# Batch 0's values loaded two rows to a partition and put in order by TensorE, in a fused sliding-window attention and feed-forward kernel

## The chip, the cores and the metric

The kernel runs on one core of a Trainium2 chip. The metric is the device time of one execution in microseconds (us). The engines are TensorE (PE in the profile; its weight loads are PEld), VectorE (DVE), ScalarE (ACT), GpSimd (POOL) and SyncE (SP), which here only issues DMAs. "SPq" is time that SP spends issuing a DMA.

## The reference

Eight batches of attention with eight heads, 576 positions and 64 values a head. A query sees keys at most 32 positions away. The result, with the heads side by side, is the input of a feed-forward block with a tanh-GELU.

```python
scores = (1/sqrt(64)) * q @ k.T                     # q, k, v: (8, 8, 576, 64) float32
scores = where(abs(pos_q - pos_k) <= 32, scores, -1e9)
attn = softmax(scores)                              # per batch and head
x = (attn @ v).transpose(0, 2, 1, 3).reshape(4608, 512)
h = x @ w_in                                        # w_in: (512, 2048)
out = gelu_tanh(h) @ w_out                          # w_out: (2048, 512)
```

## The kernel before

Heads are taken in pairs ("pair" below: heads 2g and 2g+1, g from 0 to 3), because two heads of 64 fill 128 partitions. The attention of a batch has four groups, one for each pair, and a fifth for the last positions. Everything is computed in float16 with float32 sums.

The feed-forward block works on 512 tokens at a time (stage t). Its input `xT` holds the attention's result transposed: 128 rows for each pair, so pair g of the attention is reduction block `dc = g` of the first product. `ffn_in(t, n, d0, d1)` multiplies column block n of w_in (16 blocks of 128) with reduction blocks d0 to d1; `gelu` follows; `ffn_out_0` does the second product of stage 0, in the order `ORDER_0`, 64 slots of one matmul each. While stage t runs its second product, the attention of batch t+1 is interleaved into it by slot number; for stage 0 the table is `PLAN_0`: "s" is a score, "r" a transposition of a pair, "n" sums and their inverse, "p" the product with the values, "x" the spread into xT, "w" and "u" casts of w_out's blocks, "d" shifted copies of V, "c" differences of w_out's blocks.

Queues are in order: each engine runs its instructions in the order in which the code emits them. The beginning, up to stage 0's second product, is written out by hand. SP issues nearly all loads in this order: q and k of batch 0 by pair, the tails of v (positions 512 to 575), v by head, and the eight blocks of w_in (`load_w_in(x, dc)`: half x of the columns, reduction block dc), with v's last two heads between the first blocks. Behind them come q and k of batch 1 and w_out. The loads of w_in and w_out go to five staging buffers of which batch 0's v takes one.

For batch 0 a pair goes through these steps:

- `cast_early` casts q and k, `turn` transposes both on TensorE, and `trans_out` copies them from PSUM to `QTs` and `KTs`. q and k are loaded four rows to a partition, so the keys are written with a step of four.
- `score` adds a bias of -30000 outside the window (`bias`, through matmuls with the identity `idn`), adds the scores, and takes the exponent on ACT.
- `sums_of` sums the exponents with a matmul, and ACT turns the sum into its inverse by a logarithm and an exponent (`invert`).
- `values` casts v of the pair from the load's buffer to `Vs` and `pair_v` makes two copies shifted by 64 positions, on DVE, since windows overlap two tiles of 128.
- `finish` multiplies with the values (`times`) and writes the product with the inverse to xT (`spread`).

`V` has position p of tile c at partition p, slot c, so v is loaded with one row of 64 float32 (256 bytes) for each descriptor. Between `finish(1)` and `finish(2)`, `spin` issues matmuls on a zeroed tile whose results are not used. Then `block_in` runs the first product of column blocks 0 to 5, one reduction block at a time, each after its cast (`cast_w_in`: half on POOL, half on ACT or DVE). `finish(3)` stands behind reduction block 1, and the ACT table for GELU is loaded after it.

w_out's blocks 12 to 15 are staged in two loads of two blocks. The action "w3" casts blocks 12 (DVE) and 13 (POOL) at slot 47, the action "u3" casts blocks 14 (POOL) and 15 (ACT) at slot 55. The second product reads blocks 12 and 13 from slot 48 and blocks 14 and 15 from slot 56.

## Time and profile before

| | us |
|---|---|
| median of 3 runs (lowest to highest) | 297.86 (296.98 to 298.21) |
| the profiled execution | 299.54 |
| its span, first to last instruction | 297.8 |
| TensorE busy in the span | 285.9 (96%) |
| VectorE, ScalarE, GpSimd busy | 212.8 (71%), 196.4 (66%), 89.3 (30%) |

The mean granted TensorE clock is 1.000. The chain of work that ended last is 85% TensorE, 6% DMA, 3% issues by SP and 2% VectorE. The kernel moves 51 MB; 98,471 of its 114,392 DMA packets are under 512 bytes. Times in the text are microseconds from the start of the span. A bracket behind an instruction in a listing gives the time that its engine stood idle before it, and what ended that.

### The profile page before, as it was taken

What the parts mean: (1) busy time and instruction counts of PE and PEld (TensorE: products, weight loads), DVE (VectorE), ACT (ScalarE), POOL (GpSimd) and SP (SyncE); (2) the same over time, 40 slices, a digit from 0 to 9 for tenths busy, and PEclk for the clock granted to TensorE, in tenths of its full rate; (3) what the DMA queues carried; (4) which work ended last, traced back from release to release, by engine and by line L of the source; (5) the groups of instructions that cost most, each with busy time, mean ns of one, the idle gap of its engine ahead of it and who ended that gap; (6) DMA issues with size and microseconds to landing.
All of it is one profiled execution on the core that took longest, in us unless ns stands there. A gap on an engine that the chain in (4) does not pass through costs nothing.

```text
span 297.8 us, 7286 instructions
## 1 busy us (share of the span) xinstructions
PE 285.9 (96%) x2945; PEld 192.6 (65%) x2945; DVE 212.8 (71%) x467; ACT 196.4 (66%) x315; POOL 89.3 (30%) x143
## 2 busy tenths in 40 slices
PE   7879999999999999999999999999999999999992
PEld 3434544557875687568855885588557867877781
DVE  4655378897897667868786878686857867865852
ACT  5965766778577875777667765786578558707700
POOL 3426315102347622305260615060800050024000
PEclk9999999999999999999999999999999999999999
DMA  7999999999999996999988999999693040013013
GB/s 231 235 327 412 353 310 221 257 183 193 268 240 195 262 219 130 146 130 242 163 191 132 251 117 191 111 244 155 118 147 42 2 130 12 2 36 109 0 55 89
DMA packets 114392, 51.02 MB, mean 171 GB/s; under 512 B 98471, under 2 KB 110247, under 8 KB 114102
## 3 DMA queue, kind: packets, MB, share of 16 engines
q1 hardware_dynamic: 89460, 38.67, 61.4%
q0 software_dynamic: 23776, 10.83, 23.3%
q10 hardware_dynamic: 1122, 1.06, 1.1%
q8 instruction: 23, 0.38, 0.6%
q14 instruction: 11, 0.09, 0.1%
HBM read 36.70 MB, written 9.44 MB: 155 GB/s over the span
## 4 chain that ended last, share of the span: by engine, by line
PE 85%; DMA 6%; SPq 3%; DVE 2%; ACT 1%; issue 0%; POOL 0%; ACTq 0%
PE mm L751 33%; PE ph L577 17%; PE mm L577 17%; PE ps_s L468 3%; PE pu L629 3%; DMA wst<-in_moe_w_in_dram 2%; PE ps_d L495 2%; DMA KT<-k 2%; PE mm L723 2%; PE py L723 2%; PE ps_o L505 2%; SPq L271 2%; DMA qr<-in_q_dram 1%; PE mm L629 1%; PE ps_od L495 1%; SPq L246 1%
## 5 line engine op out<-in xcount | busy, mean ns | idle before, releaser
L577 PEld LDWEIGHTS <-w_in 128*128 128x128 f16 x512 | 57.4, 113 | 50.4 <-POOL w_in L250 2.1
L577 PE MATMUL ph<-xT,w_in 128*128 128x512 f16 x256 | 64.6, 379 | 1.1 <-POOL w_in L250 1.1
L577 PE MATMUL mm<-xT,w_in 128*128 128x512 f16 x256 | 64.1, 379 | 0.0
L713 POOL DMA_DIRECT2D out_dram<-y x55 | 32.3, 597 | 84.9 <-DVE y L780 76.2
L585 ACT ACTIVATE gT<-mm 128x512 f16<-128x512 f32 x60 | 35.6, 598 | 33.1 <-PE mm L577 32.5
L751 PEld LDWEIGHTS <-s 128*128 128x128 f16 x512 | 49.3, 98 | 7.1 <-DVE s L694 0.6
L751 PE MATMUL mm<-t,s 128*128 128x256 f16 x376 | 45.2, 273 | 0.2 <-DVE y L764 0.2
L694 DVE TENSOR_TENSOR s<-gT 128x512 f16<-128x512 f16 x64 | 27.8, 435 | 19.4 <-ACT gT L585 19.3
L751 PEld LDWEIGHTS <-gT 128*128 128x128 f16 x384 | 36.2, 98 | 6.4
L585 ACT ACTIVATE gT<-ph 128x512 f16<-128x512 f32 x58 | 32.4, 604 | 11.2 <-PE ph L577 11.2
L481 ACT ACTIVATE pe<-ps_s 128x960 f16<-128x960 f32 (+1 forms) x31 | 29.6, 976 | 13.4 <-PE ps_s L468 13.3
L751 PE MATMUL mm<-w_out,gT 128*128 128x256 f16 x256 | 32.6, 273 | 0.0
L104 ACT ACT_TABLE_LOAD x18 | 23.1, 1283 | 2.2 <-issue 1.9
L530 ACT ACTIVATE lt<-ps_d 128x480 f32<-128x480 f32 (+2 forms) x28 | 15.5, 555 | 11.4 <-PE ps_d L495 7.9
L531 ACT ACTIVATE lt<-lt 128x480 f32<-128x480 f32 (+3 forms) x36 | 21.1, 586 | 1.1
L490 DVE TENSOR_TENSOR pe<-pe,band 128x960 f16<-128x960 f16 x28 | 18.1, 664 | 2.1 <-ACT pe L481 2.0
L505 PEld LDWEIGHTS <-V 128*64 128x64 f16 x520 | 13.8, 111 | 6.4 <-DVE V L226 1.6
L751 PE MATMUL mm<-t,gT 128*128 128x256 f16 x128 | 16.2, 273 | 0.0
L216 POOL DMA_DIRECT2D V<-in_v_dram x16 | 14.4, 910 | 1.3 <-POOL after L989 0.4
L694 DVE TENSOR_TENSOR s<-s,gT 128x512 f16<-128x512 f16 x32 | 13.9, 435 | 1.1
L751 PE MATMUL mm<-w_out,s 128*128 128x256 f16 x120 | 14.6, 273 | 0.0
L540 DVE TENSOR_TENSOR xT<-ps_o,lt 128x480 f16<-128x480 f32 (+5 forms) x26 | 13.4, 535 | 1.6 <-ACT w_in L250 1.1
(149 smaller groups left out, 390.7 us busy)
## 6 DMA issues: line engine op xcount, KB each, us to landing
kr<-in_k_dram SPq DMA_DIRECT2D x31, 256.0 KB, 9.7
qr<-in_q_dram SPq DMA_DIRECT2D x6, 1024.0 KB, 6.1
wst<-in_moe_w_in_dram SPq DMA_DIRECT2D x8, 512.0 KB, 7.4
wst<-in_moe_w_out_dram SPq DMA_DIRECT2D x2, 1024.0 KB, 10.6
wst<-in_moe_w_out_dram SPq DMA_DIRECT2D x4, 512.0 KB, 7.5
qr<-in_v_dram SPq DMA_DIRECT2D x8, 256.0 KB, 6.9
V<-in_v_dram POOLq DMA_DIRECT2D x16, 128.0 KB, 8.5
qr<-in_q_dram SPq DMA_DIRECT2D x7, 256.0 KB, 7.3
```

The costliest lines, as they stand in the source:

```text
L104: nc.scalar.add_instruction(mybir.InstLoadActFuncSet(name=nc.get_next_instruction_name(), act_func_set_id=which, ins=[], outs=[]))
L216: nc.gpsimd.dma_start(V[:, c, :, :], v[b, :, 128 * c:128 * c + 128, :].rearrange("h p d -> p h d"))
L481: nc.scalar.activation(pe, ps[:, :, 0:w], AF.Exp, scale=SCALE)
L490: nc.vector.tensor_tensor(pe, pe, m.rearrange("k (o j) p -> k o j p", o=1).broadcast_to(list(pe.shape)), op=ALU.mult)
L505: nc.tensor.matmul(o[64 * h:64 * h + 64, cols].rearrange("d (j p) -> d j p", j=4)[:, :, p0 - q0:p1 - q0], Vs[b % 2][:, slot, 2 * pr + h, : ...
L530: nc.scalar.activation(lt[:, 0:n], d[:, 0:n], AF.Ln)
L531: nc.scalar.activation(lt[:, 0:n], lt[:, 0:n], AF.Exp, scale=-1.0)
L577: nc.tensor.matmul(ph, w_cols[:, dc, fc // 4, fc % 4, :], xT[:, dc, t * 512 % RING:t * 512 % RING + 512], start=(dc == 0), stop=(dc == 3))
L585: nc.scalar.activation(gTs[t][:, fc, :], phs[fc], AF.Gelu_apprx_tanh)
L694: nc.vector.tensor_tensor(dst, x, y, op=op)
L713: eng.dma_start(out_v[b, j, q0 + p:q0 + p + e, cols], yo[m:m + e, cols])
L751: nc.tensor.matmul(pys["apart"][:, 0:256] if apart else py[:, blk, :], lhsT, wino[w][:, f, :], start=(new and i % (8 if one else 16) == 0) ...
```

## The change

Batch 0's v is loaded by pair in two DMAs of 128 partitions, each with two consecutive positions of a head in one partition (512 bytes). The order of SP's loads becomes pair 0, the tails, pair 1, w_in block 0, pairs 2 and 3, w_in's other blocks. The staging buffer is then out of order by position within a tile of 256 rows. POOL casts a pair to float16 in a corner of the not yet used tile `gT` (`cast_pair`), TensorE picks 32 rows at a time with a permuted identity (`pick`, eight matmuls of 256 columns, `turn_pair`), DVE copies the result from PSUM to `Vs` (`place_pair`) and makes the two shifted copies as before (`pair_of`).

The order that this leaves within each 64 positions is not the natural one, so batch 0's keys are written in the same order: `trans_out` writes runs of 16, the bias is added through a permuted 64x64 identity (`in_block`, with a separate matmul for the last eight columns), and a mask `band_0` in that order serves batch 0's last group.

The spins between `finish(1)` and `finish(2)` go. The first half of w_in's block 0 is cast by ACT inside `sums_of(3)`, the other by POOL between the casts of pairs 2 and 3. Reduction block 0 of the first product stands before `finish(2)`, block 1 is split around `finish(2)`, block 2 around `finish(3)`, and the column order of block 0 is 4, 5, 0, 2, 3, 1. The casts of w_out's blocks 12 and 13 are separate actions ("w3" at slot 41, "w4" at slot 47), "u3" goes from slot 55 to 50, and six later actions move by one to three slots.

```diff
-PLAN_0 = {... 41: "r3@1", 43: "e1 d0",
-          47: "s3@0 v-1@1 d1 w3 e2 e3", 48: "d2 m3 d3", 52: "x-1", 53: "n2@0",
-          55: "u3", 57: "p0@0 p2@1 x0 x1", 58: "e4 x2 x3", 60: "c1"}
+PLAN_0 = {... 41: "w3 r3@1", 43: "e1 d0",
+          47: "s3@0 v-1@1 d1 w4 e2 e3", 48: "d2 m3 d3", 50: "u3", 52: "x-1", 54: "n2@0",
+          59: "p0@0 p2@1 x0 x1", 60: "e4 x2 x3", 61: "c1"}
...
-    def v_of_pair(g, hs=(0, 1)):
-        for h in (2 * g + x for x in hs):
-            nc.sync.dma_start(raws[0][3][:, :, h, :], v[0, h, 0:512, :].rearrange("(c p) d -> p c d", p=128))
-
     vs(4)
-    for g in range(3):
-        v_of_pair(g)
-    for x in range(2):
-        load_w_in(0, x)
-        v_of_pair(3, (x,))
+    def v_of_pair(g):
+        for c in range(2):
+            nc.sync.dma_start(raws[0][3][:, c, 2 * g:2 * g + 2, :],
+                              v[0, 2 * g:2 * g + 2, 256 * c:256 * c + 256, :].rearrange("h (p j) d -> p h (j d)", j=2))
+    v_of_pair(0)
+    vs(4)
+    v_of_pair(1)
+    load_w_in(0, 0)
+    v_of_pair(2)
+    v_of_pair(3)
+    load_w_in(0, 1)
...
-        copy(
-            KTs[b % 2][:, pr, :].rearrange("d (p j) -> d p j", j=4),
-            ptk[:, 0:4, :].rearrange("d j p -> d p j"))
+        if b == 0:
+            copy(KTs[0][:, pr, :].rearrange("d (b j p) -> d j b p", b=8, j=4),
+                 ptk[:, 0:4, :].rearrange("d j (b p) -> d j b p", b=8))
...
-    score(0, 3, 1)
-    sums_of(2)
-    def values(g, copy):
-        hs = slice(2 * g, 2 * g + 2)
-        copy(Vs[0][:, 0:4, hs, :], raws[0][3][:, :, hs, :])
-        pair_v(0, nc.vector.tensor_copy, hs)
+    def cast_pair(g, copy):
+        copy(v16[:, g, :, :, :], raws[0][3][:, :, 2 * g:2 * g + 2, :])
+    def turn_pair(g, ps):
+        at = ps.rearrange("k (c y h d) -> k y c h d", c=2, y=2, h=2)
+        for y in range(2):
+            for half in range(2):
+                for j in range(2):
+                    p0, q0 = 64 * half + 32 * j, 64 * y + 32 * half
+                    nc.tensor.matmul(at[p0:p0 + 32, y, :, :, :], pick[:, q0:q0 + 32],
+                                     v16[:, g, :, :, 64 * j:64 * j + 64], start=True, stop=True)
+    def place_pair(g, ps):
+        nc.vector.tensor_copy(Vs[0][:, 0:4, 2 * g:2 * g + 2, :], ps.rearrange("k (c h d) -> k c h d", c=4, h=2))
...
-    values(0, nc.gpsimd.tensor_copy)
-    values(1, nc.gpsimd.tensor_copy)
-    finish(0, bank(0))
-    finish(1, bank(1))
-    spin(2, 512, s0[:, 1, :])
-    sums_of(3)
-    spin(2, 512, s0[:, 1, :])
-    values(2, nc.gpsimd.tensor_copy)
-    finish(2, s1[:, 0, :])
-    cast_w_in(0, 0, nc.gpsimd.tensor_copy, nc.scalar.copy)
-    values(3, nc.vector.tensor_copy)
-    block_in(six, 0)
+    cast_pair(0, nc.gpsimd.tensor_copy)
+    cast_vt(0)
+    turn_pair(0, at0)
+    score(0, 3, 1)
+    place_pair(0, at0)
+    pair_of(0, nc.vector.tensor_copy)
+    cast_pair(1, nc.gpsimd.tensor_copy)
+    turn_pair(1, at1)
+    sums_of(2)
+    place_pair(1, at1)
+    pair_of(1, nc.vector.tensor_copy)
+    finish(0, bank(0))
+    cast_pair(2, nc.gpsimd.tensor_copy)
+    nc.gpsimd.tensor_copy(w_in16[:, 0, 0:512], wi[0, 0][:, 0, 0:512])
+    cast_pair(3, nc.gpsimd.tensor_copy)
+    sums_of(3, nc.scalar.copy)
+    turn_pair(2, at23[:, 0, :])
+    finish(1, bank(1))
+    turn_pair(3, at23[:, 1, :])
+    place_pair(2, at23[:, 0, :])
+    pair_of(2, nc.vector.tensor_copy)
+    place_pair(3, at23[:, 1, :])
+    block_in((4, 5, 0, 2, 3, 1), 0)
     cast_w_in(0, 1, nc.gpsimd.tensor_copy, nc.scalar.copy)
-    block_in(six, 1)
-    finish(3, s1[:, 1, :])
+    block_in((0, 2, 3), 1)
+    finish(2, s1[:, 0, :])
+    pair_of(3, nc.vector.tensor_copy)
+    block_in((1, 4, 5), 1)
+    cast_w_in(0, 2, nc.gpsimd.tensor_copy, nc.scalar.copy)
     load_table(gelu_set)
-    cast_w_in(0, 2, nc.gpsimd.tensor_copy, nc.scalar.copy)
+    block_in((0, 1, 2), 2)
+    finish(3, s1[:, 1, :])
+    block_in((3, 4, 5), 2)
     cast_w_in(0, 3, nc.gpsimd.tensor_copy, nc.vector.tensor_copy)
-    block_in(six, 2, 3)
+    block_in(six, 3)
```

## The prediction

> **What bounds the kernel now.** I read the granted clock and busy shares by stretch first, then the chain of waits, then TensorE's order of time. The stretch view has start:end, the span, busy us (instruction count) of PE, PEld, DVE, ACT and POOL, then the granted clock, the DMA share and GB/s.
>
> ```profile
> 6.00:8.00 2.00, 1.77 (x34) 1.05 (x33) 0.47 (x2) 1.12 (x3) 0.61 (x1) 1.00 1.07 353
> 10.00:12.00 2.00, 2.00 (x55) 1.17 (x41) 1.16 (x4) 1.99 (x3) 1.34 (x3) 1.00 1.35 220
> 13.00:14.00 1.00, 0.83 (x26) 0.42 (x18) 0.47 (x2) 1.00 (x2) 0.07 (x1) 1.00 0.37 106
> 14.00:20.00 6.00, 4.02 (x44) 1.75 (x44) 3.73 (x7) 3.46 (x7) 2.10 (x4) 1.00 0.96 289
> 20.00:26.00 6.00, 5.37 (x38) 2.66 (x39) 4.54 (x13) 3.85 (x7) 2.90 (x5) 1.00 1.02 409
> 26.00:36.00 10.00, 10.00 (x68) 5.31 (x67) 3.40 (x8) 6.89 (x14) 4.75 (x7) 1.00 1.06 388
> 46.00:56.00 10.00, 9.24 (x123) 4.79 (x121) 7.83 (x18) 7.28 (x15) 4.37 (x8) 1.00 0.92 241
> ```
>
> The load rate follows the row length: 353 GB/s with 1 KB rows of q and k (6 to 8 us), 220 with batch 0's 256-byte rows of v (10 to 12), 409 with 4 KB rows of w_in (20 to 26). Between 13 and 14 us the DMA engines nearly stand still; while v and w_in mix (14 to 20) they give 289. The chain says what that costs:
>
> ```profile
> 10.60 0.53 SPq L271
> ...
> 11.18 1.60 SPq L246
> ...
> 14.32 7.44 DMA wst<-in_moe_w_in_dram
> ...
> 21.82 0.63 POOL w_in L250
> ...
> 22.49 0.62 PE ph L577 x2
> ```
>
> The end is set through SP's issues of v (L271), a 1.60 us issue of w_in block 0 behind them, and the landing of block 2 of w_in (7.44 us after its issue). From 22.49 us TensorE runs without a break until 47 us. Its own rows, the idle time before each in brackets:
>
> ```profile
> 18.03 0.62 PE L577 MATMUL ph<-xT,w_in 128*128 128x512 f16 x2
> ...
> 20.43 0.62 PE L577 MATMUL ph<-xT,w_in 128*128 128x512 f16 x2 [0.92 <-POOL w_in L250]
> ...
> 22.49 0.62 PE L577 MATMUL ph<-xT,w_in 128*128 128x512 f16 x2 [0.20 <-POOL w_in L250]
> ...
> 49.78 0.59 PE L723 MATMUL mm<-w_out,gT 128*128 128x512 f16 x2 [0.23 <-DVE w_out L259]
> ...
> 54.16 0.38 PE L723 MATMUL mm<-w_out,gT 128*128 128x512 f16 x1 [0.37 <-ACT w_out L259]
> ```
>
> The first product is 24 matmuls of 0.216 us (six column blocks, four reduction blocks). Its last reduction block starts at 22.49 + 6 x 0.216 = 23.78 us. After it TensorE is the bound, so what moves 23.78 moves the end. The two brackets near 50 us are waits for casts of w_out's blocks 12 and 15.
>
> **The v loads.** Eight loads of 128 KB stay eight, with 256 rows of 512 bytes each in place of 512 rows of 256. No row of the trace has 512 bytes. A 256-byte packet costs one of 16 engines 16 x 256 / 220 = 18.6 ns, a 1 KB packet 16 x 1024 / 353 = 46.4 ns. A straight line gives 27.9 ns for 512 bytes, 294 GB/s; the ends are 220 and 353. A pair's 262 KB take 0.89 us (0.74 to 1.19). The trace gives the reckoning a test: batch 0's last k load lands at 10.48 (POOL's fourth key cast starts at 10.52); v's tails (131 KB, 0.60) and pair 0 at 220 (1.19) land at 12.27, and POOL casts pair 0 at 12.24. SP issues a load when the eighth before it has landed (batch 1's first q at 19.73, as w_in block 1 lands), which never holds the new order by more than the queue does.
>
> The new order is pair 0, v's tails, pair 1, w_in block 0, pair 2, pair 3, w_in block 1. Pair 2 lands at 10.48 + 0.89 + 0.60 + 0.89 + 1.28 (w_in, 524 KB at 409) + 0.89 = 15.03. Pairs at 353 (0.74): 14.58. Pairs at 220 and w_in at the mixed 289 (1.81): 16.46. I take 15.03, as 512 lies between the two measured lengths. The standstill at 13 us goes if the 1.60 us issue was paid behind many small rows; w_in block 0 is now issued after 256-row loads and at about 9.4 us, when q's last load has landed.
>
> [...]
>
> **The values' new path.** Before, POOL casts a pair straight into V (0.61), DVE makes two shifted copies (0.29 + 0.28). Now POOL casts (0.61), TensorE reorders with 8 matmuls of 256 columns, DVE copies 128x512 from PSUM, then the two copies. The reorder: 16 value matmuls take 0.40 to 0.44 us in the trace, and eight of 0.108 one after the other with 0.17 of drain would be 1.03; I take 0.45, the 16-matmul row being narrow like these. The copy: DVE rows from PSUM are 0.42 (f16) and 0.68 (f32, 0.60 apart); 0.60, as it reads f32.
>
> Chain from pair 2's landing: cast 0.66, reorder 0.45, the pair-1 product queued behind it 0.50, spread of pair 1 0.66, copy 2 0.60, shifted copies 0.57, copy 3 0.60 (DVE's order), product 2 0.50, spread 0.69, shifted copies of pair 3 0.57, product 3 0.50, spread 0.69: 6.99, and some eight handovers of 0.05: 7.4. So xT of pair 3 is ready at 22.45. TensorE's own order agrees: reorder 3 at 17.05 (w_in's POOL half and cast 3 after cast 2, 1.9 us), block 0 from 17.5 to 18.8 (before: 18.03), half of block 1 to 19.45, product 2, the other half, block 2 around product 3, block 3 at 22.5. Against 23.78 that is 1.25 us gained; 1.7 with pair 2 at 14.58, about 0 (-0.2) with 16.46, 0.6 less if the reorder costs 1.03.
>
> **What is free and why.** The three key copies on DVE now write runs of 16 (0.68 before; 0.42 like the query copy, or unchanged): at most 0.26 each, ahead of value work that waits for loads. Eight extra 32-column bias matmuls and one for the tail mask: under 0.1 us a score, before score 3 whose exponent (13.33 now) is wanted only by the sums near 14.5. Four POOL copies of the identity and mask, some 0.3 each by the 0.29 row of the 128x128 select, fall in POOL's 1.96 us wait before 4.57; without that cover the first key cast slips by 1.2. Removed spins (0.60 x2, twice) only filled waits. ACT casts half of w_in block 0 (0.60) ahead of the last logarithm, whose inverse the pair-3 spread needs 5 us later. SP: w_in blocks come 2.5 to 3 us earlier (block 2 at 15.03 + 0.89 + 2 x 1.28 = 18.5 against 21.78), and as the queue stays full to 36 us (388 GB/s), so do w_out's.
>
> **w_out.** Block 12's cast (DVE, 0.41 at 49.32) moves ahead of batch 1's last query copy, into an idle 0.84 us; queued behind it are query, key and V copies up to the last score. Its data land at 46.75 in the old trace (POOL casts the same half at 46.78), hence about 44 to 45.5; on time. Block 15's cast moves ahead of ACT's last logarithms; its data land by 50.3 in the old trace, earlier now. Products p0 and p2 move two slots back: five w_out matmuls (1.08) instead of seven follow them, and DVE's spreads, 0.59 each, still end before the third first-product matmul of the next stage. I take 0.5 of the 0.60 in the brackets; 0 if the data stay late, 0.76 with the small 0.16 wait nearby.
>
> **Sum.** 1.2 + 0.5 = 1.7 us. The profiled execution took 299.54 us (span 297.8, 1.74 around it): 297.8 after. It lies 1.7 above the median of the runs, 297.86, so the forecast there is 296.2. Changes under 0.5% (1.5 us) this measurement hardly tells from none.
>
> **Rivals.**
> - *Gain halved.* Pair 2 lands at 16.5: mixed 512-byte and 4 KB rows run at 289 or below, as at 14 to 20 us. Then only w_out's 0.5 and some of the rest remain: 297.3. For it: the mixture is still there. Against: fewer packets.
> - *Slower: the reorder becomes the wait.* Product 1 now stands behind reorder 2 on TensorE, and so behind pair 2's landing, whereas before it needed only pair 1. In the old trace v's last load took 6.3 us from issue (13.85) to landing (about 20.15). Pair 2's second load can be issued only at about 11.0; with 6.3 it lands at 17.3, pair 3's spread ends at 24.7, 0.95 us later than now, and w_out's data are late too: 298.8; with the reorder at 1.03 as well, 299.4. The landing decides at about 16.4, or 16.9 with w_out's gain. Against: those 6.3 us had 1.1 MB ahead, this load 0.8 MB.
> - *Nothing happens.* The start gains, but a later DMA wait (batch 2's keys, 0.21 us of waiting at 223.74) takes it back: 297.8. Against: every load up to 50 us is issued by landings, so it moves along.
> - *Clock.* The clock stays at 1.00 through 14 to 20 us, spins included. Without them TensorE's longest gap in my order is under 1 us. If it halved over block 0, 1.3 us are lost: 297.5. [...]
>
> **How the numbers follow.** Forecast 0.50; gain halved 0.18; nothing or clock 0.12; slower 0.20. Forecast alone: 295.2 (1.8 and 0.76 gained, rounded) to 297.0. The range goes from 295.0 to 298.8: it holds the cases up to the slower rival's own number and leaves out its worse half and a better DMA rate. Faster by over 0.5% (under 296.4): most of the forecast, and little of the halved case, 0.50. Slower (over 299.3): the slower rival with the reorder at its dear end or pair 2 later still, 0.13. Within: 0.37.
>
> **What would show it.** Right: DMA share near 1 from 13 to 14 us; pair 2's cast at about 15.1; block 0 at 17.5; block 3 near 22.5; no bracket on w_out. Wrong: pair 2 cast after 16.4; a reorder of 1 us; TensorE waiting for DVE's V copies before products 2 and 3 by more than 0.5 us; a granted clock under 1; DVE waiting for w_out ahead of the query copy.

## The result and the profile after

The changed kernel takes 299.44 us (median of 13 runs, 298.21 to 300.33); the kernel before took 297.86 us in runs beside it (13 runs, 296.43 to 300.26). The ratio is 1.0058, 95% interval 1.0038 to 1.0078: slower by 1.6 us. (Ratios leave out executions more than 1.5% above the fastest of their kernel, and need not equal the ratio of the two medians.) The prediction said 296.2 us and a range of 295.0 to 298.8; it was wrong in sign, and the range missed. The profiled execution took 298.88 us, its span is 296.9, its mean granted clock 0.994.

The stretch view of the changed kernel (start:end, the span, busy us of PE, PEld, DVE, ACT and POOL with counts, then granted clock, DMA share, GB/s):

```profile
13.00:14.00 1.00, 0.90 (x27) 0.33 (x16) 0.95 (x4) 1.00 (x2) 0.04 (x1) 1.00 1.06 302
14.00:20.00 6.00, 4.09 (x53) 2.08 (x54) 4.02 (x9) 4.70 (x9) 2.97 (x5) 0.74 1.05 386
20.00:26.00 6.00, 5.83 (x54) 2.82 (x53) 3.93 (x12) 1.98 (x3) 2.70 (x5) 0.97 1.05 399
46.00:56.00 10.00, 10.00 (x128) 5.18 (x126) 8.25 (x18) 8.35 (x16) 3.08 (x6) 1.00 0.98 234
```

Three of the four rows are what was hoped for. The DMA engines do not stand still at 13 us (share 1.06, before 0.37), they move 386 GB/s from 14 to 20 us (before 289), and TensorE has no break from 46 to 56 us. New is the granted clock of 0.74 in the second row, ahead of its DMA share. The same view by single microseconds:

```profile
15.00:16.00 1.00, 0.00 (x0) 0.00 (x0) 0.73 (x2) 0.99 (x2) 0.13 (x1) 1.00 0.98 362
16.00:17.00 1.00, 0.47 (x12) 0.26 (x13) 0.00 (x0) 0.97 (x3) 1.00 (x3) 0.95 1.01 377
17.00:18.00 1.00, 0.85 (x24) 0.63 (x22) 0.39 (x1) 0.43 (x2) 0.69 (x3) 0.50 1.01 406
20.00:21.00 1.00, 1.00 (x6) 0.38 (x4) 0.53 (x1) 1.00 (x1) 0.55 (x1) 0.84 1.04 418
```

TensorE does nothing for the whole microsecond from 15 to 16, and about a microsecond later, at 16.91 us, its granted clock falls to 0.50 and stays there until 20.32. TensorE's order of time, GpSimd's and one row of VectorE's, each row with its start, its length and, in brackets, the idle time before it, say why it was idle:

```profile
14.54 0.41 PE L521 MATMUL ps_d<-pe,ones 128*64 128x512 f16 x2 [0.17 <-ACT pe L507]
16.53 0.40 PE L879 MATMUL ps_v<-gT 128*32 128x256 f16 x8 [1.59 <-POOL gT L871]
16.86 0.63 PE L531 MATMUL mm<-pe,V 128*64 128x96 f16 x16
17.65 0.61 PE L879 MATMUL ps_v<-gT 128*32 128x256 f16 x8 [0.15 <-POOL gT L871]
18.20 1.47 PE L603 MATMUL ph<-xT,w_in 128*128 128x512 f16 x3
...
23.31 0.44 PE L531 MATMUL ps_o<-pe,V 128*64 128x96 f16 x16
...
23.93 0.59 PE L603 MATMUL ph<-xT,w_in 128*128 128x512 f16 x2
24.61 0.59 PE L603 MATMUL ph<-xT,w_in 128*128 128x512 f16 x2
```

```profile
15.87 0.61 POOL L871 CAST gT<-vr 128x512 f16<-128x512 f32 x1 [2.83 <-DMA vr<-in_v_dram]
16.42 0.61 POOL L908 CAST w_in<-wst 128x512 f16<-128x512 f32 x1
16.98 0.61 POOL L871 CAST gT<-vr 128x512 f16<-128x512 f32 x1
```

```profile
23.86 0.69 DVE L566 TENSOR_TENSOR xT<-ps_o,lt 128x512 f16<-128x512 f32 x1 [0.70 <-PE ps_o L531]
```

The reordering of pair 2 (L879 at 16.53) stands at the head of TensorE's queue and waits 1.59 us for pair 2, whose cast begins at 15.87, as its load lands. Product 1 (L531 at 16.86) stands behind it with its own inputs ready since 15.13, when VectorE's copies of pair 1 end. Block 0 of the first product then starts at 18.20 and runs at 0.43 us a matmul instead of 0.216. The last reduction block begins at 24.61 us, the last row of TensorE's, as pair 3's spread into xT ends (23.86 + 0.69 = 24.55); the prediction had 22.5. On the good side, the waits for w_out near 50 us are gone.

One mark serves all comparisons below: the first transposition of batch 1's queries. It starts 9.06 to 9.09 us (42 matmuls) behind the last reduction block's start in the four traces where both are read here, and so shows how long the beginning took. It came at 33.05 us in the execution of the kernel before from which the prediction was worked, and here at 33.67:

```profile
33.67 0.39 PE L402 MATMUL pt<-idn,q 128*128 128x128 f16 x4
```

### The profile page after: what moved, and what is told of

It reads as the page before. It is cut to its first block, busy times and chain, and to the rows that moved or that the text cites. A ratio compares the mean times of both kernels' runs of the same rounds, so it can differ in the third digit from the quotient of the medians.

```text
span 296.9 us, 7372 instructions
## 1 busy us (share of the span) xinstructions
PE 287.6 (97%) x2982; PEld 193.8 (65%) x2982; DVE 214.4 (72%) x470; ACT 196.5 (66%) x316; POOL 89.6 (30%) x148
## 3 DMA queue, kind: packets, MB, share of 16 engines
q10 hardware_dynamic: 1122, 1.06, 1.1%
## 4 chain that ended last, share of the span: by engine, by line
PE 74%; DMA 12%; SPq 6%; DVE 4%; issue 1%; ACT 1%; POOL 0%; DVEq 0%; POOLq 0%
PE mm L777 32%; PE mm L603 15%; PE ph L603 13%; DMA kr<-in_k_dram 6%; DMA tr<-in_q_dram 3%; PE pu L655 3%; PE ps_s L494 3%; PE ps_d L521 2%; DMA wst<-in_moe_w_in_dram 2%; SPq L197 2%; PE ps_o L531 2%; DMA vr<-in_v_dram 2%; SPq L255 1%; DVE s L720 1%; PE mm L655 1%; DVE t L710 1%
## 5 line engine op out<-in xcount | busy, mean ns | idle before, releaser
L531 PEld LDWEIGHTS <-V 128*64 128x64 f16 x520 | 13.7, 113 | 4.5 <-issue 1.0
```

What stands on the lines that cost most here:

```text
L531: nc.tensor.matmul(o[64 * h:64 * h + 64, cols].rearrange("d (j p) -> d j p", j=4)[:, :, p0 - q0:p1 - q0], Vs[b % 2][:, slot, 2 * pr + h, : ...
```

## The experiments

Each run stands beside the kernel before on the same chip. "Mark" is the start of the row above, in the profiled execution of the run.

**The kernel before, again.** No edit.

> The kernel before, unchanged, for a second profile: the first profiled execution took 299.54 us against a median of 297.86, so it is not a typical one. All theories: ratio 1.00, granted clock 1.000, span near 296.1. If the waits of 0.23 and 0.37 us on w_out's casts near 50 us and the standstill of the DMA engines at 13 us are typical, they are there again; if they are what made the first execution long, they are gone or smaller.

298.10 us (12 runs; the 35 of the kernel before beside them have 297.93), ratio 1.0022, interval 0.9999 to 1.0045, as it should be. Its trace is not the one that the prediction was worked from. Stretch view, TensorE's waits (engine, tile and line, what it waited for, us in total, times, longest), and the mark:

```profile
13.00:14.00 1.00, 0.78 (x20) 0.42 (x18) 0.41 (x3) 1.00 (x2) 0.61 (x1) 1.00 1.07 327
14.00:20.00 6.00, 4.58 (x45) 2.01 (x46) 3.62 (x9) 4.52 (x8) 1.84 (x3) 1.00 1.06 348
```

```profile
PE mm L723 <- ACT w_out L259: 0.4, 1, 0.4
PE mm L723 <- DVE w_out L259: 0.3, 1, 0.3
```

```profile
31.52 0.39 PE L382 MATMUL pt<-idn,q 128*128 128x128 f16 x4
```

There is no standstill at 13 us, and SP issues w_in block 0 in 0.51 us at 10.77 in place of 1.60 (an issue of 1.40 us stands at 12.34 instead, for v's last head); 14 to 20 us move 348 GB/s in place of 289. The mark is at 31.52, 1.53 us earlier, and the last reduction block starts at 22.46 in place of 23.96. The waits for w_out are there as before. So the stall at the start, from which 1.25 us were to be gained, belongs to single executions; the waits for w_out belong to the kernel.

**The changed kernel with filler.** Six matmuls whose results are not used, in TensorE's idle stretch.

```diff
     sums_of(3, nc.scalar.copy)
+    s0 = psS.tile([128, 2, 512], FP32, name="ps_o", tag="S0")
+    spin(6, 512, s0[:, 1, :])
     at23 = psS.tile([128, 2, 512], FP32, name="ps_v", tag="S1")
     turn_pair(2, at23[:, 0, :])
```

> The changed kernel with six spins (1.3 us of matmuls on zeros) in TensorE's gap of 1.58 us ahead of the reorder of pair 2. Clock theory: the granted clock stays at 1.000 (0.994 in the changed kernel, half from 16.9 to 20.3 us), block 0 of the first product runs 0.216 us a matmul instead of 0.43, and 1.0 to 1.7 us come back: 297.7 to 298.4. Late-values theory (the time is lost to the landing of pair 2 at 15.87 and to DVE's copies behind it, and the slow clock only fills waits): the clock is mended but the time stays within 0.3 us of 299.4.

298.07 us (12 runs, 297.50 to 299.05), ratio 1.0005 (0.9985 to 1.0025); the mean clock of the twelve runs is 0.996 to 1.000, that of the changed kernel's mostly 0.994. TensorE's order of time:

```profile
14.70 1.47 PE L293 MATMUL ps_o<-KT 128*128 128x512 f16 x6
16.62 0.40 PE L879 MATMUL ps_v<-gT 128*32 128x256 f16 x8 [0.46 <-POOL gT L871]
16.96 0.44 PE L531 MATMUL mm<-pe,V 128*64 128x96 f16 x16
17.74 0.40 PE L879 MATMUL ps_v<-gT 128*32 128x256 f16 x8 [0.34 <-POOL gT L871]
18.07 0.84 PE L603 MATMUL ph<-xT,w_in 128*128 128x512 f16 x3
...
23.48 0.59 PE L603 MATMUL ph<-xT,w_in 128*128 128x512 f16 x2
...
32.54 0.39 PE L402 MATMUL pt<-idn,q 128*128 128x128 f16 x4
```

The reordering comes no earlier (16.62), block 0 hardly (18.07), but its matmuls take 0.216 us, the last reduction block starts at 23.48 and the mark is at 32.54, 1.13 us before the changed kernel's. 1.47 us of work without use more than pays: the halved clock cost 1.1 us by the traces and 299.44 - 298.07 = 1.4 us by the medians. Clock theory had 1.0 to 1.7.

**The kernel before without its filler.** Both `spin(2, 512, ...)` calls left out.

```diff
-    s0 = psS.tile([128, 2, 512], FP32, name="ps_o", tag="S0")
-    spin(2, 512, s0[:, 1, :])
     sums_of(3)
-    spin(2, 512, s0[:, 1, :])
```

> The kernel before without the four spins between the products of pairs 1 and 2. Clock theory: the clock falls here too in the stretch from 14 to 20 us (TensorE busy 4.0 of 6 us with the spins, 2.8 without) and the time grows by 0.8 to 1.7 us, ratio 1.003 to 1.006. If the fall needs the long gap of the changed kernel (1.58 us without any matmul), the clock stays at 1.000 and the ratio is 1.000: the spins were then not what the change should have kept.

298.26 us (296.97 to 299.92), ratio 1.0019 (0.9997 to 1.0042): not told from the kernel before by the time, and under the 1.003 to 1.006 of the clock theory; but its clock is 0.985 to 0.994 in 10 of 12 runs, as that theory had it. The stretch view is taken here in pieces of 3.41 us, at whose edges the granted clock changes; below it TensorE's row at the longest gap:

```profile
12.10:15.52 3.42, 2.06 (x58) 1.17 (x54) 2.71 (x7) 3.36 (x7) 1.05 (x3) 1.00 1.15 301
15.52:18.93 3.41, 2.37 (x20) 1.17 (x21) 1.26 (x3) 1.98 (x4) 1.51 (x3) 0.50 1.06 350
18.93:22.34 3.41, 3.41 (x9) 1.03 (x7) 1.00 (x3) 2.11 (x3) 1.47 (x3) 0.50 1.02 414
22.34:25.76 3.42, 3.42 (x31) 1.87 (x31) 2.64 (x10) 1.12 (x3) 1.71 (x3) 1.00 1.04 400
```

```profile
16.09 0.29 PE L505 MATMUL ps_o<-pe,V 128*64 128x96 f16 x2 [1.20 <-POOL V L844]
```

The clock is one half for 6.83 us, and no gap is longer than 1.20 us. The filler that the change takes out is what held the clock in most executions of the kernel before. It does not hold it in all: 2 of the 12 runs above, and 8 of the 35 beside them, have a mean of 0.985 to 0.994. A mean of 0.994 alone proves no fall at the start, since a fall at the end can give it too: the second trace of the run without reordering, below, where TensorE ends at 291.9 us, has a mean of 0.994 with a full clock until 294.1 us and one half for the last 3.5.

**The slot table alone.** The kernel before with the new `PLAN_0` and the split cast of blocks 12 and 13.

```diff
-PLAN_0 = {... 41: "r3@1", 47: "... d1 w3 e2 e3", 53: "n2@0", 55: "u3", 57: "p0@0 p2@1 x0 x1", ...}
+PLAN_0 = {... 41: "w3 r3@1", 47: "... d1 w4 e2 e3", 50: "u3", 54: "n2@0", 59: "p0@0 p2@1 x0 x1", ...}
...
-                    if g == 3:
-                        cast_w(wo[g], w_out16[:, 12:16, :], cs=(0, 1), on_dve=(0,))
+                    if g in (3, 4):
+                        cast_w(wo[3], w_out16[:, 12:16, :], cs=(g - 3,), on_dve=(0,))
```

> The kernel before with nothing but the new slots of the second product of stage 0 (w_out's blocks 12 and 15 cast sooner, the products with the values two slots later). My prediction's step: 0.5 us faster, ratio 0.998. DVE theory (DVE is busy without a break from the first of those products to 69 us, so that putting the products 0.43 us later puts all of it later and the waits saved on TensorE come back as a wait for DVE's query copy near 68 us): 0 to 0.4 us slower, ratio 1.000 to 1.0015.

297.38 us (296.60 to 299.59), ratio 1.0002 (0.9977 to 1.0026): by the time nothing that can be told, which is where the DVE theory had it. The trace says more. From the mark (31.46) to the second transposition of L356 (L376 after the change), in the next stage, 34.48 us pass, where the kernel before has 34.93 and 35.21 in its two traces; the changed kernel and its filled version have 34.42 both. The waits for w_out are gone, and a new one stands where TensorE had none, before that transposition:

```profile
PE pt L376 <- DVE QT L380: 0.4, 1, 0.4
```

(the changed kernel's row of waits; the slot table alone has the same 0.37 us.) VectorE is busy without a break from 53.80 us on in the changed kernel, as it is from 53.36 in the first trace of the kernel before, up to these query copies. Reckoned from the mark VectorE begins that stretch only 0.18 us sooner, since the spreads were moved two slots back, so TensorE now meets its query copies too early. The table gains 0.45 to 0.8 us net of that, by single traces.

**The values' new way alone, at a full clock.** The filled version with the old slot table (the diff above turned round).

> The changed kernel with the six filler products that kept the clock in the earlier run, and with the slot table and the single w3 cast of the kernel before: the values' new way alone, at a full clock. If the new way of the values costs 0.8 to 1.0 us by itself and the slot table gains 0.6, this run gives 298.7 to 298.9 us beside some 297.9 for the kernel before, the last reduction block of the first stage starts near 23.2 us and the two waits for w_out (0.27 and 0.37 us) are back near 48 and 53 us. If the slot table does nothing, it gives the 298.1 us of the run with the new table. If the values' way is free and only the clock made the loss, it gives about 297.9.

298.73 us (297.95 to 300.00) beside 297.72 for the kernel before, ratio 1.0030 (1.0007 to 1.0052); clock 0.996 to 1.000, mark 33.08, 34.95 us from it to the later transposition, the waits for w_out are back. The values' way costs about 1.0 us (0.2 to 1.5 by the interval) at a full clock, and the slot table is worth 298.73 - 298.07 = 0.7 us by the medians; the intervals of the two ratios overlap, so that the times alone do not show it. With the clock's 1.4 this makes 1.0 + 1.4 - 0.7 = 1.7, where 1.6 was measured. That is no test of the three parts: they are differences of the same few medians, and their sum comes out near the whole by itself.

**Loads of pair 2 ahead of w_in's block 0.** No filler.

```diff
-    load_w_in(0, 0)
     v_of_pair(2)
+    load_w_in(0, 0)
     v_of_pair(3)
```

> The changed kernel with the loads of value pair 2 issued ahead of w_in's block 0, without any filler. Late-values theory (pair 2 stands behind 512 KB of w_in in the stream, and everything after it follows): its cast starts near 14.7 us in place of 15.87, the 1.58 us gap of TensorE before product 1's chain shrinks below 0.6, the granted clock stays at 1.00 from 14 to 20 us, the last reduction block starts at 22.5 to 22.9 us and the time is 297.2 to 297.8 us. Clock-by-mean-load theory (the clock falls because TensorE is busy for too small a share between 10 and 17 us, wherever the longest gap is): the gap shrinks but the clock still halves, and the time stays over 298.6 us. Rival on the loads: block 0 of w_in now lands 0.8 us later and becomes the wait at the first reduction block, which then starts no earlier than 18.2 us.

299.59 us (298.83 to 300.70), ratio 1.0068 (1.0045 to 1.0091). Late-values theory failed in its main point; the theory of the mean load had the halved clock and the time over 298.6 us. TensorE, then GpSimd's cast of pair 3:

```profile
15.79 0.40 PE L879 MATMUL ps_v<-gT 128*32 128x256 f16 x8 [0.82 <-POOL gT L871]
16.12 0.44 PE L531 MATMUL mm<-pe,V 128*64 128x96 f16 x16
17.91 0.40 PE L879 MATMUL ps_v<-gT 128*32 128x256 f16 x8 [1.35 <-POOL gT L871]
18.25 0.98 PE L603 MATMUL ph<-xT,w_in 128*128 128x512 f16 x3
```

```profile
17.25 0.62 POOL L871 CAST gT<-vr 128x512 f16<-128x512 f32 x1 [0.24 <-DMA vr<-in_v_dram]
```

Pair 2's cast begins at 15.12, 0.75 us earlier than in the changed kernel's trace. The loads as a whole were later in this execution: reckoned from pair 0's cast (11.55 here, 10.95 there) pair 2 comes 1.35 us earlier, for 524 KB less ahead of it. The gap is not closed but cut in two, and its larger part (1.35 us) is now at pair 3, which lands at 17.25, after w_in's block 0 (16.39). The clock halves from 18.81 us. Block 0 starts where it did.

**Block 0 ahead of pair 3's reordering.** The filled version with three products of block 0 put forward.

```diff
-    turn_pair(3, at23[:, 1, :])
     place_pair(2, at23[:, 0, :])
     pair_of(2, nc.vector.tensor_copy)
-    place_pair(3, at23[:, 1, :])
...
-    block_in((4, 5, 0, 2, 3, 1), 0)
+    block_in((4, 5, 0), 0)
+    turn_pair(3, at23[:, 1, :])
+    place_pair(3, at23[:, 1, :])
+    block_in((2, 3, 1), 0)
```

> The changed kernel with the six filler products and with three products of reduction block 0 moved ahead of the reordering of pair 3, so that TensorE does not wait for pair 3's cast on GpSimd first. If the reordering that stands in front is what delays block 0, the 0.34 us wait goes, block 0 starts at 17.3 to 17.5 us in place of 18.07 and the time is 297.4 to 297.7 us in place of 298.07. If the values' chain (the cast of pair 2 at 15.96 and what follows on VectorE) sets the last reduction block, it still starts near 23.2 us and the time stays at 298.0 us, with a wait ahead of product 2 or 3 in place of the one removed.

298.82 us (298.33 to 299.76), ratio 1.0033 (1.0016 to 1.0051). The wait for GpSimd went, and a longer one took its place:

```profile
19.26 0.40 PE L879 MATMUL ps_v<-gT 128*32 128x256 f16 x8 [0.68 <-DVE V L883]
```

Pairs 2 and 3 share a PSUM tile, and pair 3's reordering now had to wait until VectorE had copied pair 2 out of it. That is the edit's own fault, so the run does not settle the question of the queue's order; it was asked again below.

**The slot table with more filler.** The run with the slot table alone, with one filler matmul ahead of `finish(1)` and three in place of two ahead of `finish(2)`.

```diff
-    finish(1, bank(1))
     s0 = psS.tile([128, 2, 512], FP32, name="ps_o", tag="S0")
+    spin(1, 512, s0[:, 1, :])
+    finish(1, bank(1))
     spin(2, 512, s0[:, 1, :])
     sums_of(3)
-    spin(2, 512, s0[:, 1, :])
+    spin(3, 512, s0[:, 1, :])
```

> The kernel before with the new slot table and the split w3 cast alone, and with two more filler products, one ahead of the first attention's product 1 and one ahead of product 2, each in the place of a 0.39 us wait. If the slot table gains 0.6 us and the scatter of that run alone (296.6 to 299.6 us) came from executions with a lower clock in the first stage, this gives 296.6 to 297.0 us with a granted clock of 0.996 or more in nearly all executions, under both kernels. If the lower clock comes from elsewhere, the scatter and the median of 297.4 us stay.

297.98 us with a wide scatter, 296.04 to 302.36, ratio 1.0005 (0.9975 to 1.0034). The clock is 0.992 to 1.000, yet the scatter is larger than ever, so it is not the clock's alone. The profiled execution (clock 0.999, mark 33.90) shows another cause. GpSimd and TensorE:

```profile
17.48 0.62 POOL L250 CAST w_in<-wst 128x512 f16<-128x512 f32 x1 [1.97 <-DMA wst<-in_moe_w_in_dram]
```

```profile
18.16 0.62 PE L577 MATMUL ph<-xT,w_in 128*128 128x512 f16 x2 [0.76 <-POOL w_in L250]
```

The loads were slow in this execution: 216 to 286 GB/s from 14 to 20 us, where the kernel before had 348 in its second trace. Block 0's wait of 0.76 us is followed by two more for blocks 1 and 2. No version here beats the kernel before by what can be measured.

**Where the 1.0 us of the values' way comes from.** The remaining runs have the DMA transposes of batches 1 to 3 replaced by plain copies of the same size (their queries and keys are then in the wrong order), so they compare only with each other. The edit common to all, for the queries:

```diff
-        nc.sync.dma_start_transpose(QTs[b].rearrange("d r j p -> d (r j) p")[:, :, p0:p1],
-                                    dst.rearrange("p r j h d -> p (r j h d)"))
+        flat, n = dst.rearrange("p r j h d -> p (r j h d)"), p1 - p0
+        for i in range(128 // n):
+            nc.sync.dma_start(QTs[b].rearrange("d r j p -> d (r j) p")[n * i:n * i + n, :, p0:p1],
+                              flat[:, 16 * n * i:16 * n * i + 16 * n].rearrange("p (a x) -> p a x", a=16))
```

The changed kernel so:

> The changed kernel, as the anchor of this set of four. All four have the DMA transposes of batches 1 to 3 (queries, keys and their tails, all issued after the first stage) replaced by plain DMA copies of the same number of bytes, so the queries and keys of those batches are not in the reference's order and their attention is computed on other data; the first stage is untouched, and the times compare within the set only. Expected: TensorE's idle stretch of about 1.6 us ahead of the reordering of pair 2, the granted clock at about 0.5 for some 3.4 us from 16 to 20 us, the last reduction block of the first stage (the sixth product on w_in's fourth row block after product 3) at 24.4 to 24.7 us.

300.52 us (298.60 to 301.45). Pair 2's cast begins at 16.30 and TensorE's gap is 2.04 us in the profiled one; the clock halves, the mark is at 34.58. Two of the eleven runs have a clock of 0.997 and 0.998, and 299.05 and 298.60 us; the nine others, 0.988 to 0.994, have a median of 300.53.

Product 1 ahead of pair 2's reordering, no filler:

```diff
+    finish(1, bank(1))
     at23 = psS.tile([128, 2, 512], FP32, name="ps_v", tag="S1")
     turn_pair(2, at23[:, 0, :])
-    finish(1, bank(1))
     turn_pair(3, at23[:, 1, :])
```

> The anchor of this set (plain copies in place of the DMA transposes) with the first attention's product 1 ahead of the reordering of pair 2, as the values of pair 1 are there by 15.0 us while pair 2's cast ends near 16.5; no filler. Gap theory (one long idle stretch of 1.58 us makes the clock fall): product 1 parts the gap, its longest piece is near 1.1 to 1.2 us, and the clock stays at 1.00: 1.2 to 1.6 us under the anchor. Load theory (a share of busy time over several microseconds makes it fall, whatever the pieces): the clock still halves, and the time is within 0.4 us of the anchor's. By either, block 0 starts no earlier than 18.0 us, because the reordering of pair 3 still stands ahead of it and waits for GpSimd.

300.65 us (298.58 to 302.03), within 0.13 us of its anchor. In 11 of 12 runs the clock is 0.984 to 0.994; the profiled one is the twelfth: gaps of 0.33, 1.12 and 0.71 us, a clock of 1.00 from 10 to 24 us (mean 0.998), mark 32.59 and 298.58 us. So, by the means and the times, the same program keeps the clock in one execution and loses it in eleven. Gap theory, which had it kept, fails; load theory, with the time within 0.4 us of the anchor's, fits.

Filler, product 1 first, and two products of block 0 ahead of pair 3's reordering, pair 3 with a tile of its own:

```diff
+    finish(1, bank(1))
+    s0 = psS.tile([128, 2, 512], FP32, name="ps_o", tag="S0")
+    spin(4, 512, s0[:, 1, :])
+    at2 = psS.tile([128, 2, 512], FP32, name="ps_v", tag="S1")
+    turn_pair(2, at2[:, 0, :])
...
+    block_in((0, 2), 0)
+    at3 = psS.tile([128, 2, 512], FP32, name="ps_v", tag="S0")
+    turn_pair(3, at3[:, 0, :])
+    place_pair(3, at3[:, 0, :])
+    block_in((3, 1, 4, 5), 0)
```

> The anchor of this set with four filler products, product 1 ahead of the reordering of pair 2, and the first two products of reduction block 0 ahead of the reordering of pair 3, which has a tile of its own now, so that it does not wait for VectorE's copy of pair 2 as it did (0.68 us) in the run that moved block 0 alone. Queue-order theory (the 0.9 us that the values' way costs at a full clock come from work that stands behind a reordering on TensorE's queue): block 0 starts at 17.0 to 17.2 us in place of 18.07, the last reduction block at 22.7 to 22.9 in place of 23.2, and the time is 1.7 to 2.0 us under the anchor's (1.3 of it the clock). Landing theory (pair 2 and pair 3 come too late, and the order can give back no more than 0.1 us): 1.2 to 1.4 us under the anchor, with a new wait for VectorE's values ahead of product 2 or 3.

299.32 us (298.46 to 300.05), 1.20 us under its anchor: what the clock gives, and no more. Block 0 started at 17.59 (17.0 to 17.2 in queue-order theory), but its fifth product waits:

```profile
19.81 0.81 PE L606 MATMUL ph<-xT,w_in 128*128 128x512 f16 x3 [0.71 <-DVE V L886]
```

VectorE has to copy pair 3 out of the tile that this product needs. The same, with the loads of pair 2 ahead of w_in's block 0 as well:

> As the run before it (fillers, product 1 and block 0 put forward), and with the loads of value pair 2 ahead of w_in's block 0 as well. If both the order on TensorE's queue and the order of the loads are what costs the values' way its 0.9 us, this is the changed kernel at its best: pair 2's cast near 15.1 us, block 0 at 17.0 to 17.3, the last reduction block at 22.3 to 22.6, and 2.0 to 2.4 us under the anchor. If w_in's later landing takes it back, block 0 or block 1 waits for the cast of w_in and the time is no lower than that of the run before it.

299.68 us (298.38 to 301.18). Pair 2's cast begins at 15.04, but product 1 now waits 0.84 us for VectorE and block 0 starts at 17.78, its fifth product at 19.86. Queue-order theory finds no support in either run: what is put forward on TensorE waits for VectorE's copies, in part because the tiles for the reordering take PSUM that block 0 needs.

Last, the reordering itself taken out of the filled version, between two anchors:

```diff
-        copy(v16[:, g, :, :, :], raws[0][3][:, :, 2 * g:2 * g + 2, :])
+        copy(Vs[0][:, 0:4, 2 * g:2 * g + 2, :].rearrange("p (a b) h d -> p a b (h d)", a=2), raws[0][3][:, :, 2 * g:2 * g + 2, :])
...
-    turn_pair(0, at0)
-    place_pair(0, at0)
...
-    turn_pair(3, at23[:, 1, :])
-    place_pair(2, at23[:, 0, :])
```

(and so for the other pairs).

> The kernel before with the DMA transposes of batches 1 to 3 replaced by plain copies of the same size (their queries and keys are not in the reference's order), as the lower anchor of this set. The changed kernel became 1.1 us longer by that replacement (300.52 beside 299.44); if the replacement costs the same here, this gives 298.6 to 299.2 us.

299.78 us (297.49 to 302.19): the lower anchor is no anchor, its scatter is too wide. In its profiled execution the clock halves as well, after a gap of 0.96 us with one of 0.39 us behind it, fillers and all.

> The changed kernel with the six filler products that kept the clock, and with the plain copies: the upper anchor of this set at a full clock. With the DMA transposes it had 298.07 us, level with the kernel before; here 298.8 to 299.3 us, within 0.4 us of the lower anchor, block 0 near 18.0 us and the last reduction block near 23.2.

298.95 us (298.54 to 299.84). The profiled execution is the longest of the twelve, mark 33.87.

> The upper anchor without the reordering: the values still come two rows to a partition, but are cast straight into their place, so that the rows of batch 0's values are in the wrong order, and the 32 products that reorder them on TensorE and VectorE's four copies out of PSUM (0.67 to 0.69 us each) are left out. Chain theory (the 0.9 us that the values' way costs at a full clock is the reordering itself, cast to copy to product, 0.33 + 0.69 us on the path and 2.7 us more of VectorE): block 0 starts at 17.1 to 17.4 us, the last reduction block at 22.2 to 22.5, and the time is 0.7 to 1.0 us under the upper anchor, which is what the loads and the slot table alone would give. Landing theory (pairs 2 and 3 and w_in's block 0 simply land too late): the last reduction block stays at 23.0 us or later and the time within 0.3 us of the upper anchor.

300.22 us (299.31 to 302.72), 1.3 us over the upper anchor where the chain theory had 0.7 to 1.0 under it. Its mark is at 33.42, 0.45 us before the anchor's. Both were run again:

> The upper anchor of the set before, unchanged, again: the changed kernel with six filler products and with plain copies in place of the DMA transposes of batches 1 to 3. Its profiled execution there was 0.9 us over its own median (298.95 us). Expected: 298.7 to 299.2 us, and a first stage that ends (first transposition of batch 1) near 33.0 us.

> The run without the reordering, unchanged, again (the rows of batch 0's values are in the wrong order; the 32 products and VectorE's four copies out of PSUM are left out). It was 1.3 us longer than the upper anchor, where the chain theory had it 0.7 to 1.0 us shorter, but a good 1 us of its profiled execution lies at the very end, after the last output transfer is issued. If leaving the reordering out gives nothing (landing theory), the first stage ends within 0.3 us of the anchor's. If the chain theory holds for the first stage and the end is another matter, the first stage ends 0.6 us or more before the anchor's, whatever the total time is. If the total is again over 300 us, the end is a property of this kernel and not of one execution.

298.97 us (298.60 to 299.70) and 299.61 us (298.85 to 300.34). The marks, the filled version first, then the one without reordering, and TensorE's waits in the latter:

```profile
33.06 0.39 PE L402 MATMUL pt<-idn,q 128*128 128x128 f16 x4
```

```profile
17.54 0.41 PE L606 MATMUL ph<-xT,w_in 128*128 128x512 f16 x1 [0.41 <-POOL w_in L905]
...
19.02 0.41 PE L606 MATMUL ph<-xT,w_in 128*128 128x512 f16 x1 [0.44 <-POOL w_in L251]
...
32.36 0.39 PE L402 MATMUL pt<-idn,q 128*128 128x128 f16 x4
```

Without the reordering the mark comes 0.70 us sooner (0.45 in the first pair), and TensorE waits for the casts of w_in's blocks 0 and 1 in place of the values. Block 0's cast stands on GpSimd behind pair 2's, which begins at 16.30, so the late landing is still in the way. Four traces of filled versions, all with the same first stage, have the mark at 32.54, 33.06, 33.08 and 33.87: a difference of 0.45 to 0.70 between single traces shows little by itself. But in three of the four, and in the profiled execution with product 1 first, the mark stands 16.58 or 16.59 us behind the start of pair 2's cast (15.96 to 16.50); in the fourth 17.09. At a full clock the landing of pair 2 and a chain of fixed length thus set the mark in these forms. Without the reordering the distance is 16.77 and 16.06.

The times contradict a gain, because the end is longer. From the end of the last addition on VectorE to the end of the span, the two runs without reordering have 5.45 and 5.30 us, the two anchors 4.30 and 4.26. Why is open: the first trace of the kernel before has 5.12 there, its second 4.24, so single executions differ in this too, but the medians differ by 0.6 and 1.3 us the same way.

So how the 1.0 us divides is known only by single traces. The two quick traces of the kernel before's first stage (its second one and that of the slot table alone) have pair 2's cast at 15.59 and 15.48 and the mark 15.93 and 15.98 us behind it. Against them the filled version's landing of 15.96 to 16.50 is 0.4 to 1.0 us later, and its chain 0.6 us longer. What the order on TensorE's queue could give back did not show in the forms tried.

## Why the prediction was wrong

**The execution it was worked from.** The sum took 1.2 us from a start that held a standstill of the loads and an issue of 1.60 us, and then set the forecast as far below the median as below that execution. The second trace has neither the standstill nor that issue; its last reduction block starts at 22.46, just where the change was predicted to bring it (22.45 to 22.5). The profiled execution's 1.7 us over the median were there to be read as a warning. Beside the second trace it is 1.53 us longer before the mark, in the part to be improved, 0.88 longer after the last addition, and 1.1 shorter between. Beside such an execution the start could have gained nothing, even with every term of the chain right. Nor was 23.78 the start of the last reduction block: TensorE stood there for 0.15 us until the cast of w_in's block 3 ended at 23.90, and the block began at 23.96.

**The loads (pair 2 lands at 15.03, 14.58 to 16.46).** Its cast begins at 15.87, and at 15.96 to 16.78 in the ten other traces with this order of loads. The rate was not the error: 302 GB/s from 13 to 14 us and 386 from 14 to 20 are above the 294 taken. The queue was: the sum let one load land after the other. From pair 0's cast to pair 2's (10.95 to 15.87 us) the engines moved 337 GB/s, 1.66 MB, where the sum's four loads have 1.18. The trace's packets say what the rest was: by 15.87 all but 2 of the 2048 rows of v had been begun, pair 3's with them, and 240 rows of w_in, where block 0 has 128. The 1.28 us for w_in's block 0 were not too much: with pair 2 ahead of it, pair 2's cast follows pair 0's by 3.30 and 3.57 us in place of 4.79 to 5.27. So pair 2 came later than in the kernel before (14.66 to 15.59 in six traces) and only pair 3 sooner (16.98 in place of 19.02 to 21.24). What 512-byte rows do by themselves cannot be read from these runs.

**The chain from that landing (7.4 us).** Right, at a full clock: 15.96 to 23.48 is 7.5 us in the filled version. The reorder took 0.40 us (taken 0.45), the copy out of PSUM 0.67 to 0.69 (taken 0.60), a key copy 0.41 (taken 0.42). With the landing 0.9 us late the last reduction block came 1.0 us late.

**The filler that "only filled waits".** This step failed, and it is the largest term: 1.4 us. "TensorE's longest gap in my order is under 1 us" followed from the landing at 15.03; it was 1.59. The rival "clock" had the price right (1.3 us), and of its chance too little: it shared 0.12 with "nothing happens". Its ground against was the stage's full clock, spins included; that the clock was full because of the spins could have been weighed from the rows, two pieces of 0.60 us in a stretch where TensorE was busy 4.02 of 6 us. That a gap under 1 us leaves the clock as it is was the author's estimate, and no trace showed it: in the kernel before with plain copies the clock fell behind gaps of 0.96 and 0.39 us.

In the five traces in which the granted clock falls in the first stage, it falls at 15.52, 15.8, 16.91, 17.9 and 18.81 us, stands at 0.50 for 3.41 us (in the first, the kernel before without its filler, for 6.83), and is 1.00 again. In the changed kernel's trace the next fall, at 296.80 us, comes 276.48 us behind the rise at 20.32, which is 81 times 3.413. Stretches of that length, laid on from the edges of each trace, of the changed kernel (two), of its filled version (one), and of the one execution that kept the clock with product 1 first (two):

```profile
13.49:16.91 3.42, 1.57 (x32) 0.77 (x32) 2.18 (x6) 3.36 (x7) 1.04 (x2) 1.00 1.10 355
16.91:20.32 3.41, 3.26 (x33) 1.46 (x31) 2.65 (x5) 2.17 (x4) 1.93 (x4) 0.50 1.01 406
...
12.57:15.98 3.41, 2.99 (x58) 1.56 (x50) 2.90 (x7) 3.35 (x7) 0.61 (x2) 1.00 1.12 337
...
12.66:16.07 3.41, 2.14 (x68) 1.49 (x59) 3.29 (x8) 3.35 (x7) 0.67 (x2) 1.00 1.08 327
16.07:19.49 3.42, 2.10 (x23) 1.08 (x23) 1.49 (x5) 1.65 (x3) 2.28 (x4) 1.00 1.00 387
```

In the stretch just before the fall TensorE was busy for 0.35 of the time in the changed kernel with plain copies, 0.46 in the changed kernel, 0.49 with pair 2's loads put forward, 0.51 in the kernel before with plain copies and 0.60 in the kernel before without its filler; the longest gaps were 0.96 to 2.04 us. In the 14 others the clock stays at 1.00 from 10 to 24 us. The stretches shown of them have 0.88, 0.63 and 0.62, the thinnest of the first trace of the kernel before has 0.65 (14.31 to 17.73 us); but in the first run without reordering TensorE is busy for 0.56, 0.94, 0.00 and 0.90 us of the four microseconds from 17 on, 0.60 of the time, and the clock holds, so the share alone does not part them. With product 1 first, the gaps lay on both sides of 16.07, with 0.63 and 0.62 in the two stretches, and the clock stayed. That its eleven other runs fell because their stretches lay otherwise is the author's estimate and not shown: they have no trace.

**"Slower: the reorder becomes the wait."** Product 1 did stand behind reorder 2 with ready inputs, for 1.4 us of the idle stretch, as that rival had it, but its price came by another way: at a full clock the queue's order cost nothing that the runs show, and the idle stretch took the clock. Its point of decision, a landing at 16.4, was not reached here; in two filled traces at 16.47 and 16.50 the mark is at 33.06 and 33.08, level with the 33.05 that the prediction started from, as that rival had it.

**w_out (0.5 us; 0 to 0.76).** Right: both waits are gone, 0.45 to 0.8 us by the traces (0.2 at the least, in the one with more filler), 0.7 by the medians, which the intervals do not tell from nothing. "p0 and p2 two slots later are harmless" was almost right: a wait of 0.36 us for VectorE's query copy came in its place, and is in the net.

**Key copies, GpSimd's extra copies, bias matmuls.** Costed at nothing; no wait for any of them shows in TensorE's rows after.

Of the 1.6 us, then, by the medians: +1.4 the clock, +1.0 the values' way, -0.7 the slot table. The first is clear of the noise (the intervals 1.0038 to 1.0078 and 0.9985 to 1.0025 do not meet), the second just so, the third is not.

## What to carry to other kernels

A profiled execution that is longer than the median of its kernel is not the kernel: what is to be gained must be in a second trace too, above all a stall of the loads. Filler matmuls in a thin stretch of TensorE may be what keeps its clock; a change that takes them out, or makes TensorE wait longer there, has to be priced with what a fall took here: a clock of 0.50 for 3.41 us, in one trace for 6.83. In these traces the falls went with TensorE's busy share over the 3.41 us before them (0.35 to 0.60, against 0.62 to 0.88 in the stretches shown where the clock held) more than with the longest gap: the clock fell behind one of 0.96 us and held behind one of 1.12. And work put ahead of a wait on one queue pays only if nothing else, here the PSUM copies on VectorE (waits of 0.68 and 0.71 us), sets the same time.

## What the runs showed that was not expected

- In five traces the granted clock fell to 0.50 behind 3.41 us in which TensorE was busy for 0.35 to 0.60 of the time, and stayed there for 3.41 us, in one for 6.83. Whether it falls varies from execution to execution: with product 1 put forward, 11 of 12 have a mean of 0.984 to 0.994, the twelfth 0.998.
- The first stage's loads vary much between executions of one program: the mark came at 31.46, 31.52, 33.05 and 33.90 us in four traces at a full clock with the 256-byte rows of v, at 32.54, 33.06, 33.08 and 33.87 in four with 512-byte rows and filler. The kernel before scatters from 296.55 to 301.81 us in 34 runs, the filled version with the old slot table, beside it, from 297.95 to 300.00. With 12 runs beside 34 and four traces beside four, it is not shown that the longer rows make the start steadier; no trace has it earlier with them.
- From the last addition to the end of the span, 4.0 to 5.5 us pass, and which it is does not follow from the edits made.
